# Attention and feed-forward on one core: copies of normalised rows issued last in their slot, raw heads in a head's first slot, v a slot later

## The chip, the cores and the metric

The kernel runs on one core of one Trainium2 chip. The metric is the device time of one execution in microseconds (us); lower is better. A core has five engines that run at the same time and meet through semaphores: TensorE (PE, matrix products; its weight loads are listed as PEld), VectorE (DVE), ScalarE (ACT), GpSimd (POOL) and SyncE (SP), which here issues every DMA, in the order in which the program lists them. If the next DMA in SP's list has to wait for a semaphore, all those behind it wait too.

## The reference

Decaying causal attention for 8 batches of 8 heads (576 tokens, head size 64), followed by a feed-forward block on the normalised rows:

```python
scores = scale * np.matmul(q, k.transpose(0, 1, 3, 2))
cum = np.cumsum(np.log(np.clip(f, 0.0001, 1.0)), axis=-1)
decay = cum[:, :, :, None] - cum[:, :, None, :]
scores = np.where(causal, -1000000000.0, scores + decay)
attn = np.exp(scores - np.max(scores, axis=-1, keepdims=True))
attn = attn / (np.sum(attn, axis=-1, keepdims=True) + 1e-09)
x = np.matmul(attn, v)          # then heads side by side: 4608 rows of 512
xn = (x - mu) / np.sqrt(var + 1e-06) * g_ln
out = x + np.maximum(xn @ w_ch1, 0.0) @ w_ch2
```

`w_ch1` and `w_ch2` come as float64. Everything else is float32.

## The kernel before

**Slots.** The 64 heads are worked off in 256 slots, four to a head: slot (n, t), with t from 1 to 4, computes the scores of one block of 128 query rows of head n (t = 1 takes the 64 rows ahead of it as well). A slot is a string of letters, and each letter is a piece of program: the list `ORDERS` (L53) gives the order for slots 0 to 36, 37 to 69 and from 70 on. Since every engine runs its own instructions in program order, this string also sets the order on each engine's queue. From slot 70 on it reads `WwDAthQFlMSPNgreamLRB`.

**What the letters issue.** `Q` is the score product (PE); `S` takes scores from PSUM into a row buffer `p` and finds the row extreme (DVE, L398); `e` is the exponential (ACT, L409); `B` divides the rows by their sums (two small DVE instructions, L414 and L415, then POOL, L416). `D` calls `move` (L426): from head 18 on SP copies the normalised rows of the slot before from `p` to a buffer `pq`, 32 to 288 KB a copy, five copies to a head (L431). `t`, `h` and `l` transpose the rows of the slot four before (PE), and split them into a high and a low part (ACT, DVE; L492, L497); heads below 18 do it two slots after. `A` multiplies them with v (PE, L527), one slot after the transposes; `F` and `a` add the halves and send the result to DRAM (L574). `M`, `r`, `m` and `N` are one step of the feed-forward: `M` the first product (PE, L604 to L606), `r` the Relu (ACT, L612), `m` its low part (DVE, L617), `N` the second product of the step before (PE, L626 to L628). `R` loads and splits what the feed-forward needs next: pieces of x (`xr`, split in L588 and L589) and rows for the residual (`xw`), all from L637; in some slots that is a train of eight and more DMAs. `N` also sends finished rows out (L687). `W`, `w`, `g` and `L` are pieces of the weights' preparation (in the first slots) and of small row statistics. Ahead of the letters, each slot loads the low part of a piece of the second weight (`w2s`, L719).

**What `P` issues** (`prep`, L867). In slot (n, t) it prepares head n + 1: t = 1 loads two rows of `kl` and rounds the raw k on ACT (L341, in `prep_a`); t = 2 subtracts on POOL (L344) and rounds the raw q on ACT (L348); t = 3 copies 64 rounded rows to `xq` by DMA (L351) and subtracts on POOL (L352). In slot (n, 4) it loads the raw q and k of head n + 2 (`start_head`, L323, 576 KB, from head 8 on; two buffers in turn). In the slot in which a head's first rows are transposed it rounds that head's v on DVE and POOL (`prep_v`, L358 and L359, from head 12 on), and right behind that it loads the next head's v (`load_v`, L331, 160 KB; from head 12 on into one and the same buffer, below that into two in turn).

**Buffers that matter here.** The row buffer `p` has three copies, one to a slot, so DVE's L398 writes a buffer again three slots after it was filled; it must then have been copied to `pq`. `pq` has nine.

**Overlap.** The feed-forward runs beside the attention from slot 35 on as far as rows and weights are there; what is left of its 288 steps runs alone when the heads are done, from about 1040 us on.

Of the kernel before, what the change touches and what calls it, by code (L numbers as in the profile page):

```python
# [15 lines left out]
B, H, S, D = 8, 8, 576, 64  # L16
# [10 lines left out]
NPLAIN = 8  # L27
# [25 lines left out]
ORDERS = [  # L53
    (0, "WwbQsSthAeMrgFmlLNPaRf"),
    (37, "WwbQSstAMhPelgLNFrfmBRa"),
    (70, "WwDAthQFlMSPNgreamLRB"),
]


# [1 line left out]
def attn_moe(ctx: ExitStack, tc: tile.TileContext, qk, v, f, g, w1, w2, out):  # L61
# [264 lines left out]
    def load_v(h):  # L326
        if h.full and h.n % 2 == 1:
            h.vr = work.tile([P, 5, 2, D], F32, tag="vv", bufs=1, name=f"vr{h.n}")[:, :, 0, :]
        else:
            h.vr = work.tile([P, 5, D], F32, tag="vr", bufs=1, name=f"vr{h.n}")  # L330
        nc.sync.dma_start(out=h.vr, in_=v[h.n])  # L331
# [31 lines left out]
    def qk_mm(h, t):  # L363
        q0, m, w = QT[t]
        cuts = [(0, w)] if w <= 512 else [(0, w // 2), (w // 2, w)]
        h.s = getattr(h, "s", {})
        h.s[t] = []
        for i, (a, z) in enumerate(cuts):
            sp = bank(f"s{h.n}_{t}_{i}")[:m, : z - a]
            xq, kl = h.xq[:, q0 : q0 + m], h.kl[:, a:z]  # L370
            if h.plain:
                mm(sp, xq, kl, start=True, stop=True)
            else:
                mm(sp, h.hi[:, 0, q0 : q0 + m], h.hi[:, 1, a:z], start=True, stop=False)  # L374
                mm(sp, xq, kl, start=False, stop=True)  # L375
            h.s[t].append((a, z, sp))
# [11 lines left out]
    def softmax_a(h, t):  # L388
        q0, m, w = QT[t]
        nm = f"{h.n}_{t}"  # L390
        if t == 0:
            pt = corner(h.n)
        else:
            pt = work.tile([P, S], F32, tag="p", bufs=3, name=f"p{nm}")
        st = work.tile([P, 4], F32, tag="st", bufs=6, name=f"st{nm}")
        off = S - P - (w - m)
        for i, (a, z, sp) in enumerate(h.s[t]):
            nc.vector.tensor_tensor_reduce(  # L398
                out=pt[:m, a:z], in0=sp, in1=mask[:m, off + a : off + z], scale=-SCALE,
                scalar=3.0e38 if i == 0 else st[:m, 0:1], op0=ALU.add, op1=ALU.min, accum_out=st[:m, i : i + 1],  # L400
            )
        h.p = getattr(h, "p", {})
        h.p[t] = (pt, st)

    def softmax_e(h, t):
        q0, m, w = QT[t]
        pt, st = h.p[t]
        i = len(h.s[t]) - 1
        nc.scalar.activation(pt[:m, :w], pt[:m, :w], AF.Exp, bias=st[:m, i : i + 1], scale=-1.0, accum_out=st[:m, 2:3])  # L409
# [80 lines left out]
    def transposed_hi(h, t):  # L490
        for tp, hi, lo in h.parts:
            nc.scalar.copy(out=hi, in_=tp)  # L492

    def transposed_lo(h):
        if not h.full:
            for tp, hi, lo in h.parts:
                nc.vector.tensor_tensor(out=lo, in0=tp, in1=hi.bitcast(F32), op=ALU.subtract)  # L497
# [50 lines left out]
    def finish(h):  # L548
        po, w, c0 = h.o
        b, hh = divmod(h.n, H)  # L550
        pr, j = divmod(hh, 2)
        g1 = c0 == 0
        if j == 0:
            xs_tile[g1] = work.tile([P, w], F32, tag="xs1" if g1 else "xs2", bufs=1, name=f"xs{h.n}_{c0}")
        xs = xs_tile[g1]
        js = slice(64 * j, 64 * j + 64)
        if h.full:
            nc.scalar.copy(out=xs[js, :], in_=po[0:64, :w])
        else:
            tmp = late.tile([P, S1], F32, tag="ot", bufs=1, name=f"ot{h.n}_{c0}")  # L560
            nc.scalar.copy(out=tmp[js, :w], in_=po[64:128, :w])
            h.tmp = tmp
        h.xs = xs

    def finish_add(h):
        po, w, c0 = h.o
        b, hh = divmod(h.n, H)
        pr, j = divmod(hh, 2)
        g1, xs = c0 == 0, h.xs
        js = slice(64 * j, 64 * j + 64)  # L570
        if not h.full:
            nc.vector.tensor_tensor(out=xs[js, :], in0=po[0:64, :w], in1=h.tmp[js, :w], op=ALU.add)
        if j == 1:
            nc.sync.dma_start(out=(xd1 if g1 else xd2)[b][P * pr : P * pr + P, :], in_=xs)  # L574
# [198 lines left out]
    hd = {}  # L773

    def start_head(n):
        hd[n] = load(n)
# [9 lines left out]
    for u, slot in enumerate(slots):  # L786

        def before(k):
            return slots[u - k] if u >= k else None

        if slot is not None:
            n, t = slot
            h = hd[n]
        def turn(more):

            for lag in (LAG, LAG_MOVED):
                b = before(lag + more)
                if b is not None and hd[b[0]].lag == lag:
                    return b
            return None  # L800

        av, av_t = None, 0
        if turn(1) is not None and turn(1)[1] in (2, 4):
            av, av_t = hd[turn(1)[0]], turn(1)[1]
        moe.fetch_low(ALL if wp.done() else wp.ready())
        want = moe.can(wp.ready()) and u >= FIRST_MOE

        def piece(c):
            tu = turn(0)
            if c == "t" and tu is not None:  # L810
                transpose_unit(hd[tu[0]], tu[1])
            elif c == "h" and tu is not None:
                transposed_hi(hd[tu[0]], tu[1])
            elif c == "l" and tu is not None:
                transposed_lo(hd[tu[0]])
            elif c == "Q" and slot is not None:
                if t == 1:
                    qk_mm(h, 0)
                qk_mm(h, t)
            elif c == "A" and av is not None:  # L820
                av_unit(av, av_t)
            elif c == "S" and slot is not None:
                if t == 1:
                    softmax_a(h, 0)
                softmax_a(h, t)
            elif c == "e" and slot is not None:
                if t == 1:
                    softmax_e(h, 0)
                softmax_e(h, t)
            elif c in FILL:  # L830
                wp.fill(FILL[c])
            elif c == "s":
                wp.sums()
            elif c == "F" and av is not None:
                finish(av)
            elif c == "a" and av is not None:
                finish_add(av)
            elif c == "r" and want:
                moe.first_high()
            elif c == "R":  # L840
                moe.limit = min(NCHUNK, max(0, u - (LAG if u < 4 * MOVED else LAG_MOVED) - 1) // (4 * H) * S // C)
                moe.rest()
            elif c == "L":
                run_later(RSTD)
            elif c == "M" and want:
                moe.first()
            elif c == "B" and slot is not None:
                normalise(h, t)
            elif c == "D":
                if before(1) is not None and hd[before(1)[0]].n >= MOVED:  # L850
                    move(hd[before(1)[0]], before(1)[1])
            elif c == "b" and before(1) is not None:
                b_n, b_t = before(1)
                if not hd[b_n].normal.get(b_t):
                    normalise(hd[b_n], b_t)
            elif c == "m" and want:
                moe.first_low()
            elif c == "W":
                due = 1 + min(u, W_CHANGE) / W_SLOTS + max(0, u - W_CHANGE) * W_TICKS
                while not wp.done() and wp.tick_no <= due:  # L860
                    wp.tick()
            elif c == "N":
                moe.second()
            elif c == "P":
                prep()

        def prep():  # L867

            if slot is not None:
                if t == 1 and n + 1 < NPLAIN:  # L870
                    start_head(n + 1)
                if NPLAIN <= n + 1 < B * H:
                    if t == 1:
                        prep_a(hd[n + 1])
                    if t == 2:
                        prep_b(hd[n + 1])
                    if t == 3:
                        prep_c(hd[n + 1])
                if t == 4 and NPLAIN <= n + 2 < B * H:
                    start_head(n + 2)  # L880
            first = turn(0)
            if first is not None and first[1] == 1:
                m = first[0]
                if not hd[m].full:
                    prep_v(hd[m])
                if m + 1 < B * H:
                    load_v(hd[m + 1])

        for c in [o for first, o in ORDERS if first <= u][-1]:
            piece(c)  # L890
# [48 lines left out]
```

## Time and profile before

| what | value |
|---|---|
| median of 3 runs | 1246.01 us (1243.95 to 1248.18) |
| the profiled execution | 1246.79 us, of which its span is 1245.0 us |
| mean granted TensorE clock | 0.982 |
| PE busy | 1203.7 us (97% of the span) |
| PEld, weight loads | 1069.0 us (86%) |
| DVE / ACT / POOL busy | 756.8 / 642.3 / 426.0 us |
| DMA | 228.5 MB, mean 184 GB/s |

How to read what follows. A row of waits says who waited for whom, with the total in us, the number of waits and the longest. A row of the timeline has its start in us from the span's start, its length in us, the engine, the line of the kernel, the operation, what it writes and reads, and in brackets the idle time of the engine just before it and what ended that. SPq is SP's queue: such a row is the issue of a DMA, not the transfer. A row of the windows has a stretch, its length, the busy time and count of instructions of each engine, the granted clock of PE as a share of full speed, the DMA engines' share and the rate.

### The profile page before, as it was taken

How to read it: one execution, taken by the hardware profiler on the slowest of the kernel's cores; microseconds unless marked ns; L12 is line 12 of the kernel's file. 1: busy time of each engine (PE TensorE's matmuls, PEld its weight loads, DVE VectorE, ACT ScalarE, POOL GpSimd, SP SyncE). 2: the span in 40 equal slices, each digit the busy share in tenths (PEclk: the TensorE clock that was granted, in tenths of full speed). 3: DMA queues.
4: the chain of work that ended last, by engine and by line, in shares of the span. 5: the costliest groups of instructions: out<-in, count | busy, mean ns of one | idle time of the engine just before them, and what ended most of it. 6: DMA issues, size and time to landing. Idle time of an engine off the chain costs nothing.

```text
span 1245.0 us, 26040 instructions
## 1 busy us (share of the span) xinstructions
PE 1203.7 (97%) x8140; PEld 1069.0 (86%) x8140; DVE 756.8 (61%) x2884; ACT 642.3 (52%) x1920; POOL 426.0 (34%) x533
## 2 busy tenths in 40 slices
PE   7998999999999989999999999999989999999998
PEld 5666889888898879889999989998989999999997
DVE  5777646575767666566767676766666774233232
ACT  5887655455555555455555565555545553112111
POOL 3667534333343334233434443443434330000000
PEclk8998999899999999989999999999999999999999
DMA  6888554356666656556667666766666654434433
GB/s 172 247 247 255 176 161 153 99 162 200 212 203 199 192 171 215 175 187 202 217 191 222 205 207 196 221 187 209 209 182 215 199 190 132 130 125 118 153 111 93
DMA packets 171482, 228.51 MB, mean 184 GB/s; under 512 B 40784, under 2 KB 107856, under 8 KB 171344
## 3 DMA queue, kind: packets, MB, share of 16 engines
q1 hardware_dynamic: 171344, 226.85, 59.2%
q8 instruction: 65, 1.06, 0.4%
q14 instruction: 73, 0.60, 0.2%
HBM read 157.46 MB, written 23.36 MB: 145 GB/s over the span
## 4 chain that ended last, share of the span: by engine, by line
PE 52%; DMA 5%; DVE 2%; ACT 2%; SPq 1%; issue 1%; DVEq 0%; ACTq 0%; POOLq 0%; POOL 0%
PE h L605 7%; PE h L604 7%; PE h L606 7%; PE acc L626 7%; PE acc L627 7%; PE acc L628 7%; DMA raw<-in_qk_dram 4%; PE o L527 4%; PE s L374 2%; PE tr L440 2%; PE s L375 2%; ACT p L409 1%; SPq L637 1%; DMA xr<-xb 1%; PE xp L649 0%
## 5 line engine op out<-in xcount | busy, mean ns | idle before, releaser
L416 POOL TENSOR_SCALAR p<-p,st 64x64 f32<-64x64 f32 (+4 forms) x320 | 173.4, 544 | 530.4 <-DVE st L415 226.0
L604 PE MATMUL h<-x,w1h 128*128 128x256 f32 x1152 | 331.3, 288 | 6.1 <-ACT x L588 3.3
L605 PE MATMUL h<-x,w1h 128*128 128x256 f32 x1152 | 327.3, 284 | 1.2 <-DVE st L414 0.7
L606 PE MATMUL h<-x,w1l 128*128 128x256 f32 x1152 | 326.4, 283 | 0.0
L617 DVE SCALAR_TENSOR_TENSOR hh<-h,hh 128x256 fp32r<-128x256 f32 x288 | 121.2, 421 | 222.6 <-ACT hh L612 217.5
L612 ACT ACTIVATE hh<-h 128x256 fp32r<-128x256 f32 x288 | 110.4, 383 | 268.5 <-PE h L606 265.1
L626 PE MATMUL acc<-w2h,hh 128*128 128x512 f32 x576 | 229.1, 398 | 12.8 <-ACT hh L612 12.8
L604 PEld LDWEIGHTS h<-x,w1h 128*128 128x128 f32 x1152 | 219.9, 191 | 12.2 <-ACT x L588 4.4
L627 PE MATMUL acc<-w2s,hh 128*128 128x512 f32 x576 | 228.2, 396 | 0.0
L628 PE MATMUL acc<-w2h,hh 128*128 128x512 f32 x576 | 226.8, 394 | 0.0
L605 PEld LDWEIGHTS h<-x,w1h 128*128 128x128 f32 x1152 | 220.3, 191 | 6.2 <-DVE x L589 2.7
L606 PEld LDWEIGHTS h<-x,w1l 128*128 128x128 f32 x1152 | 220.3, 191 | 0.0
L409 ACT ACTIVATE p<-p,st 64x64 f32<-64x64 f32 (+4 forms) x320 | 178.3, 558 | 73.4 <-DVE st L398 64.5
L492 ACT CAST ph<-tr 64x128 fp32r<-64x128 f32 (+4 forms) x416 | 117.7, 332 | 103.4 <-PE tr L440 53.2
L398 DVE CUSTOM_DVE_ANT_0 p<-s,mask 64x64 f32<-64x64 f32 (+4 forms) x320 | 130.4, 420 | 14.0 <-PE s L375 4.0
L626 PEld LDWEIGHTS acc<-w2h,hh 128*128 128x128 f32 x576 | 110.1, 191 | 26.6 <-ACT hh L612 14.0
L628 PEld LDWEIGHTS acc<-w2h,hh 128*128 128x128 f32 x576 | 109.3, 190 | 25.1 <-DVE st L414 0.5
L627 PEld LDWEIGHTS acc<-w2s,hh 128*128 128x128 f32 x576 | 110.3, 192 | 11.9
L497 DVE TENSOR_TENSOR ph<-tr,ph 64x192 fp32r<-64x192 f32 x208 | 62.6, 301 | 92.1 <-ACT ph L492 65.4
L374 PE MATMUL s<-hi 128*64 128x64 f32 x336 | 106.4, 339 | 0.3 <-DVE st L398 0.3
L375 PE MATMUL s<-kl,xq 66*64 66x64 f32 x336 | 98.6, 298 | 0.7 <-DMA xq<-hi 0.7
L497 DVE TENSOR_TENSOR pl<-tr,ph 128x128 fp32r<-128x128 f32 x208 | 95.2, 458 | 4.6
(86 smaller groups left out, 1796.0 us busy)
## 6 DMA issues: line engine op xcount, KB each, us to landing
w2s<-w2d SPq DMA_DIRECT2D x288, 256.0 KB
raw<-in_qk_dram SPq DMA_DIRECT2D x56, 576.0 KB
wr<-in_w_dram SPq DMA_DIRECT2D x32, 512.0 KB
pq<-p SPq DMA_DIRECT2D x46, 288.0 KB
pq<-p SPq DMA_DIRECT2D x46, 224.0 KB
vr<-in_v_dram SPq DMA_DIRECT2D x64, 160.0 KB
out_dram<-xt SPq DMA_DIRECT2D x36, 256.0 KB
xq<-hi SPq DMA_DIRECT2D x56, 144.0 KB
```

What stands on the lines that cost most here:

```text
L374: mm(sp, h.hi[:, 0, q0 : q0 + m], h.hi[:, 1, a:z], start=True, stop=False)
L375: mm(sp, xq, kl, start=False, stop=True)
L398: nc.vector.tensor_tensor_reduce(out=pt[:m, a:z], in0=sp, in1=mask[:m, off + a : off + z], scale=-SCALE, scalar=3.0e38 if i == 0 else st[: ...
L409: nc.scalar.activation(pt[:m, :w], pt[:m, :w], AF.Exp, bias=st[:m, i : i + 1], scale=-1.0, accum_out=st[:m, 2:3])
L416: nc.gpsimd.tensor_scalar(out=pt[:m, :w], in0=pt[:m, :w], scalar1=st[:m, 3:4], scalar2=1.0, op0=ALU.mult, op1=ALU.mult)
L497: nc.vector.tensor_tensor(out=lo, in0=tp, in1=hi.bitcast(F32), op=ALU.subtract)
L604: mm(ph, w1h[:, k, fs], c.x[k][:, 0, :], start=(k == 0), stop=False)
L605: mm(ph, w1h[:, k, fs], c.x[k][:, 1, :], start=False, stop=False)
L606: mm(ph, w1l[:, k, fs], c.x[k][:, 0, :], start=False, stop=(k == KT - 1))
L626: mm(c.acc[i], h[:, 0, ts_], w2h[:, j, :], start=(j == 0), stop=False)
L627: mm(c.acc[i], h[:, 0, ts_], low, start=False, stop=False)
L628: mm(c.acc[i], h[:, 1, ts_], w2h[:, j, :], start=False, stop=(j == FT - 1))
```

## The change

Three things are moved; no instruction is added or taken away. The letter `D` goes from third place to the last but one, behind `R`, so that SP issues a slot's copies of normalised rows behind that slot's other DMAs. The load of the raw heads goes from slot (n, 4) to slot (n, 1), from head 10 on, behind `prep_a`. The load of the next v goes one slot further back, out of the slot that rounds the current one.

```diff
-    (70, "WwDAthQFlMSPNgreamLRB"),
+    (70, "WwAthQFlMSPNgreamLRDB"),
...
-                if t == 4 and NPLAIN <= n + 2 < B * H:
+                if t == (4 if n + 2 < NPLAIN + 2 else 1) and NPLAIN <= n + 2 < B * H:
                     start_head(n + 2)
             first = turn(0)
             if first is not None and first[1] == 1:
                 m = first[0]
                 if not hd[m].full:
                     prep_v(hd[m])
-                if m + 1 < B * H:
-                    load_v(hd[m + 1])
+            second = turn(1)
+            if second is not None and second[1] == 1 and second[0] + 1 < B * H:
+                load_v(hd[second[0] + 1])
```

`turn(0)` is the slot whose rows are transposed now, `turn(1)` the one before it.

## Prediction

> **What bounds the kernel now.** I began with the page's chain of waits, to see whether anything but TensorE (PE) carries the end.
>
> ```profile
> PE 52%; DMA 5%; DVE 2%; ACT 2%; SPq 1%; issue 1%; DVEq 0%; ACTq 0%; POOLq 0%; POOL 0%
> PE h L605 7%; PE h L604 7%; PE h L606 7%; PE acc L626 7%; PE acc L627 7%; PE acc L628 7%; DMA raw<-in_qk_dram 4%; PE o L527 4%; PE s L374 2%; PE tr L440 2%; PE s L375 2%; ACT p L409 1%; SPq L637 1%; DMA xr<-xb 1%; PE xp L649 0%
> ```
>
> PE carries it, and the largest entry that is no matmul is the load of the raw heads: 4% of 1245 us, about 50 us. Next I asked who waits for that load, and what PE itself waits for: two answers of the waits view (total us, times, longest).
>
> ```profile
> ACT hi L341 <- DMA raw<-in_qk_dram: 82.7, 39, 6.5
> ```
>
> ```profile
> PE acc L626 <- ACT hh L612: 12.8, 6, 3.2
> PE tr L442 <- POOL p L416: 7.8, 5, 2.4
> PE h L604 <- ACT x L588: 3.3, 4, 2.2
> PE h L604 <- DVE st L414: 2.8, 1, 2.8
> PE o L527 <- DVE ph L497: 2.6, 4, 1.4
> ```
>
> ScalarE (ACT) waits 82.7 us for raw heads, but PE stops only now and then. The timeline shows how the one becomes the other.
>
> ```profile
> 516.17 0.43 SPq L637 DMA_DIRECT2D xw<-xb  x1
> ...
> 517.19 0.47 SPq L431 DMA_DIRECT2D pq<-p  x1
> ...
> 517.71 0.59 SPq L323 DMA_DIRECT2D raw<-in_qk_dram  x1
> ...
> 525.11 0.67 ACT L341 CAST hi<-raw 128x576 fp32r<-128x576 f32 x1 [6.50 <-DMA raw<-in_qk_dram]
> ...
> 526.25 0.80 PE L626 MATMUL acc<-w2h,hh 128*128 128x512 f32 x1 [3.07 <-ACT hh L612]
> ```
>
> The SP queue comes to the raw load late, behind a train of xw loads and a copy of normalised rows. The load takes 7.4 us (517.71 to 525.11). ACT stands at the cast, which is queued ahead of the Relu (L612), and PE stops 3.07 us for that Relu. All six L626 stops stand like this, just behind an ACT wait for raw; here are the first and the last of them:
>
> ```profile
> 322.38 0.67 ACT L341 CAST hi<-raw 128x576 fp32r<-128x576 f32 x1 [4.35 <-DMA raw<-in_qk_dram]
> 323.51 0.50 PE L626 MATMUL acc<-w2h,hh 128*128 128x512 f32 x1 [0.28 <-ACT hh L612]
> ```
>
> ```profile
> 919.45 0.67 ACT L341 CAST hi<-raw 128x576 fp32r<-128x576 f32 x1 [5.37 <-DMA raw<-in_qk_dram]
> 920.59 0.50 PE L626 MATMUL acc<-w2h,hh 128*128 128x512 f32 x1 [3.14 <-ACT hh L612]
> ```
>
> Last, the stages: those with such stops, and one quiet stretch (556 to 735) as the yardstick.
>
> ```profile
> core 0: us, PE busy (x) PEld busy (x) DVE busy (x) ACT busy (x) POOL busy (x), PEclk, DMA share, GB/s
> 235.00:250.00 15.00, 12.22 (x68) 10.70 (x66) 6.69 (x24) 6.91 (x21) 5.18 (x7) 0.77 0.32 103
> 250.00:330.00 80.00, 77.11 (x540) 69.38 (x539) 54.49 (x218) 44.14 (x135) 30.15 (x39) 1.00 0.61 185
> 390.00:412.00 22.00, 17.88 (x116) 15.67 (x114) 15.05 (x58) 11.06 (x36) 8.91 (x11) 0.92 0.63 191
> 450.00:465.00 15.00, 11.54 (x82) 10.06 (x80) 8.18 (x33) 6.79 (x22) 4.81 (x7) 1.00 0.58 181
> 520.00:535.00 15.00, 11.81 (x64) 9.91 (x62) 7.56 (x31) 6.61 (x20) 4.80 (x6) 0.77 0.51 161
> 535.00:556.00 21.00, 18.39 (x114) 16.62 (x113) 13.81 (x54) 10.27 (x32) 6.96 (x9) 0.84 0.62 192
> 556.00:735.00 179.00, 178.93 (x1302) 164.88 (x1301) 123.86 (x495) 105.37 (x319) 70.76 (x89) 1.00 0.67 210
> 840.00:860.00 20.00, 18.03 (x133) 16.21 (x132) 11.79 (x46) 9.94 (x32) 6.36 (x8) 1.00 0.71 213
> 915.00:927.00 12.00, 8.86 (x54) 7.82 (x54) 6.38 (x26) 5.38 (x17) 4.93 (x7) 0.86 0.65 202
> ```
>
> In the quiet stretch PE is never idle and starts 1302/179 = 7.27 matmuls per us. In the others it starts fewer, and five of them also show a granted clock of 0.77 to 0.92.
>
> **The change, part by part.**
>
> *Raw heads in slot 1.* The same 56 loads; from head 10 on each is issued three slots earlier, in front of that slot's R loads. The cast then finds its data, and the ACT wait goes. What PE lost to it I count twice. By named stops: the six L626 stops, 12.8; the L604 stop behind DVE, which in the first of these stages follows such an ACT wait too, 2.8; the longest of L604 behind x, 2.2, and the longest of L527, 1.4, both in stages with a late raw head: 19.2 us. To that the clock: 15 x 0.23 + 22 x 0.08 + 15 x 0.23 + 21 x 0.16 + 12 x 0.14 = 3.5 + 1.8 + 3.5 + 3.4 + 1.7 = 13.9 us, since the low clock stands only in stages with stops. Together 33 us. By rate: each stage's length less its matmuls over 7.27: 5.6 + 5.7 + 6.0 + 3.7 + 6.2 + 5.3 + 1.7 + 4.6 = 38.8 us. That is the most that these stages can give back; 33 is what raw heads explain.
>
> [...]
>
> What is next late there? The load writes a buffer that GpSimd (POOL) last read for the head two before. It is free long before the new place, as slot (32, 3) and the issue in the first slot of head 33 show, so SP should not stand on it:
>
> ```profile
> 509.07 1.43 POOL L352 TENSOR_TENSOR hi<-raw,hi 64x576 fp32r<-64x576 f32 x1
> ...
> 519.83 0.39 SPq L340 DMA_DIRECT2D kl<-cumd  x1
> ```
>
> *Copies last in their slot.* The 230 copies (46 heads, five each) remain; each is moved on SP past the slot's kl, raw, v, xq, xs, out and R issues. SP no longer stands on POOL with these behind it.
>
> ```profile
> SPq L431 <- POOL p L416: 226.5, 134, 7.2
> ...
> SPq L331 <- POOL vv L359: 57.8, 36, 5.5
> ...
> SPq L331 <- PE o L505: 28.9, 9, 7.5
> ```
>
> The first row's 226.5 us do not become a gain: SP is not the bound, and what it held back shows in PE's stops. I add 1 us for x loads that come earlier (L604 behind x, 3.3 less the 2.2 counted). The price: a copy must land before VectorE (DVE) writes that row buffer again, three slots after it was filled. How long does a copy take? It moves 32 to 288 KB. The nearest rows are a 576 KB load without a crowd, and an x piece of at most 128 KB behind a train of loads:
>
> ```profile
> 796.14 0.58 SPq L323 DMA_DIRECT2D raw<-in_qk_dram  x1
> ...
> 800.04 0.67 ACT L341 CAST hi<-raw 128x576 fp32r<-128x576 f32 x1 [1.07 <-DMA raw<-in_qk_dram]
> ```
>
> ```profile
> 841.07 0.43 SPq L637 DMA_DIRECT2D xr<-xa  x1
> ...
> 843.13 0.41 ACT L588 CAST x<-xr 128x256 fp32r<-128x256 f32 x1 [3.14 <-DMA xr<-xa]
> ```
>
> So 2.1 to 3.9 us; I take 2.5, near the smaller, whose size is nearer. Time left for it, from the end of the slot's last SP issue to the DVE write, in a common slot and in the tightest that I found:
>
> ```profile
> 578.09 0.42 SPq L637 DMA_DIRECT2D xr<-xa  x1
> ...
> 583.52 0.61 DVE L398 CUSTOM_DVE_ANT_0 p<-s,mask 128x448 f32<-128x448 f32 x1
> ```
>
> ```profile
> 593.26 1.57 SPq L637 DMA_DIRECT2D xr<-xa  x1
> ...
> 595.81 0.48 DVE L398 CUSTOM_DVE_ANT_0 p<-s,mask 128x320 f32<-128x320 f32 x1
> ```
>
> 5.0 us and 1.0 us. In the tight slots DVE would wait 1.5 us (up to 2.9). Of the 184 slots with copies I found four with under 2.5 us left. Part of such a wait hides, as most ACT waits for raw do, so I charge half: 4 x 1.5 / 2 = 3 us; at 3.9 us a copy, some 6 us.
>
> *v one slot later.* The 64 loads leave SP after the readers of their buffer are done, so the second and third row above (86.7 us of SP) mostly vanish. v is used a whole head later, so it stays covered; were that cover gone, the rounding on DVE would wait a load of 160 KB, 2 to 4 us, in each of 52 heads. No gain is charged: after 250 us it is inside the 33, and in the weight-preparing first 120 us, where transposes wait for POOL (7.8 us above), it may be worth -3 to +4.
>
> **Sum.** 33 + 1 - 3 = 31, with the early part's middle of +0.5 some 32 us. The profiled execution took 1246.8 us (span 1245.0): 1246.8 - 32 = 1214.8. The median of the runs is 0.8 lower, so 1214. With the bounds: 33 + 1 - 6 - 3 = 25 gives 1221; 38.8 + 4 - 1 = 42 gives 1204.
>
> **Rivals.** *Half of it: the trains of loads take raw's place.* The stops of 390 to 412, 520 to 556, 840 to 860 and 915 to 927 us come where SP issues eight or more xw and xr loads in a row at 0.43 us and more each. If x pieces and copies, now behind these trains, are late as the raw heads were, only the other stages give (5.6 + 5.7 + 3.7 = 15 us): 1231. For: L604 already waits for x. Against: its total is 3.3 us.
>
> *Slower: row buffers come free too late.* In slot 1 the copy now follows 576 KB of raw head. If it took 8 us, as the load at 517.71 nearly did, DVE would miss the 5.0 us of a common slot by 3 in each of 46 heads. ACT waits average 2.1 us (82.7/39) while PE stopped in only few of them, so 2 us hide; 46 x 1 = 46 us against the gain of 33: 13 slower, 1259. It decides from 7.7 us a copy. Against: raw has 3.9 us in quiet, and SP reaches it before it stands on POOL. [...]
>
> *Nothing: SP stands on the raw buffer in slot 1, or the stops were the trains' alone.* Then loads wait as now and the time stays within 3.7 us (0.3%, about what a measurement of this kernel can tell from no change).
>
> **Chances.** Forecast, 1204 to 1223: 0.72. Half, 1224 to 1238: 0.15. More than the stages' count: 0.03. Nothing: 0.04. Slower: 0.06. So faster 0.90, same 0.04, slower 0.06. From 1203 to 1231 holds the forecast and half of the second case: 0.8.
>
> **What would show it.** Right: L341 behind raw falls from 82.7 to under 5 us; L626 behind hh from 12.8 to under 3; the clock in 500 to 560 us is 1.00; SP's waits for vv and o are near nothing; SP still waits for POOL at L431. A new DVE wait at L398 for pq copies should total under 15 us. Wrong: that wait above 50 us, SP waiting at L323 for POOL, or the stops staying with xr or xw named.

## The result, and the profile after

The changed kernel takes 1206.21 us (median of 4 runs, 1205.75 to 1206.35), the kernel before 1244.98 us on the same chip. The ratio is 0.9696, 95% interval 0.9652 to 0.974: 38 us less, where 32 had been forecast and 1214 us named. (Gains here and below are one less the ratio, times 1245 us; the two medians differ by 38.8.) The profiled spans are 1245.0 before and 1204.0 after.

The page's chain of waits of the changed kernel:

```profile
PE 92%; DVE 3%; ACT 2%; DMA 2%; issue 1%; SPq 0%; POOL 0%; DVEq 0%; ACTq 0%; POOLq 0%
PE h L604 11%; PE h L605 11%; PE h L606 11%; PE acc L626 11%; PE acc L627 11%; PE acc L628 11%; PE o L527 6%; PE s L374 4%; PE tr L440 4%; PE s L375 3%; PE o L505 3%; PE tr L442 2%; PE s L372 2%; PE xp L649 1%; PE pc L191 1%
```

The load of the raw heads has gone from the chain. The chain is now PE for 92%, where it was 52%. What PE still waits for, in the changed kernel (total us, times, longest):

```profile
PE tr L442 <- POOL p L416: 6.0, 5, 2.3
...
PE h L605 <- DVE st L414: 1.3, 2, 1.1
...
PE o L527 <- DVE ph L497: 0.6, 2, 0.4
```

The row that stood first before, L626 behind the Relu with 12.8 us, is absent, and no row of ACT's waits names the cast behind a raw load. The first row is from the first 120 us. The rows of DVE and SP on which the prediction had set its marks:

```profile
DVE p L398 <- DMA pq<-p: 5.2, 4, 3.3
```

```profile
SPq L431 <- POOL p L416: 108.2, 77, 3.2
...
SPq L331 <- POOL vv L359: 17.7, 18, 1.5
SPq L331 <- PE o L505: 6.6, 4, 3.9
```

DVE does wait for a copy to leave its row buffer now, in four places and for 5.2 us. SP still stands on POOL at the copies, for half of what it was, and for v 24.3 us instead of 86.7; at the raw load (L323) it waits once, for 0.3 us. Two of the marks were missed: the waits for v are not near nothing, and the clock in 500 to 560 us is 0.97 and not 1.00, since 515 to 535 us still has a low stretch (below). Nor does SP stand much less in all: its waits add up to 681 us before and 650 after, since its wait for DVE at L574, where the attention's results go out, grew from 28.0 to 117.3 us.

Where the time came from can be read off one instruction that both kernels have in every head: ACT's cast of the raw k. Before, for heads 15, 18, 36, 53 and 63:

```profile
201.40 0.67 ACT L341 CAST hi<-raw 128x576 fp32r<-128x576 f32 x1 [0.77 <-DMA raw<-in_qk_dram]
256.93 0.67 ACT L341 CAST hi<-raw 128x576 fp32r<-128x576 f32 x1 [1.40 <-DMA raw<-in_qk_dram]
559.92 0.67 ACT L341 CAST hi<-raw 128x576 fp32r<-128x576 f32 x1
830.47 0.67 ACT L341 CAST hi<-raw 128x576 fp32r<-128x576 f32 x1
998.82 0.67 ACT L341 CAST hi<-raw 128x576 fp32r<-128x576 f32 x1 [1.41 <-DMA raw<-in_qk_dram]
```

And after, for the same heads:

```profile
197.95 0.68 ACT L341 CAST hi<-raw 128x576 fp32r<-128x576 f32 x1
246.87 0.68 ACT L341 CAST hi<-raw 128x576 fp32r<-128x576 f32 x1
529.48 0.67 ACT L341 CAST hi<-raw 128x576 fp32r<-128x576 f32 x1
798.28 0.67 ACT L341 CAST hi<-raw 128x576 fp32r<-128x576 f32 x1
956.96 0.67 ACT L341 CAST hi<-raw 128x576 fp32r<-128x576 f32 x1
```

The lead grows from 3.5 us (201.40 - 197.95) to 10.1, 30.4, 32.2 and 41.9. Between heads 36 and 53, 270 us in which PE had hardly stopped before, it grows by 1.8 us; all the rest falls in the stretches with stops. Those stretches now run at the pace of the quiet ones, but for one (windows of the changed kernel):

```profile
250.00:330.00 80.00, 79.56 (x570) 73.01 (x568) 58.57 (x229) 47.63 (x145) 34.60 (x44) 1.00 0.65 205
500.00:515.00 15.00, 14.88 (x103) 13.07 (x101) 13.09 (x55) 9.20 (x31) 6.33 (x8) 1.00 0.67 212
515.00:535.00 20.00, 18.39 (x116) 16.37 (x117) 12.86 (x52) 10.39 (x32) 8.41 (x12) 0.91 0.75 245
535.00:700.00 165.00, 165.00 (x1204) 152.34 (x1203) 115.24 (x452) 97.53 (x295) 66.06 (x83) 1.00 0.67 210
```

570/80 = 7.1 and 1204/165 = 7.3 matmuls per us; only 515 to 535 us is left at 5.8.

### The profile page after: what moved, and what is told of

It reads as the page before. It is cut to its first block, busy times and chain, and to the rows that moved or that the text cites. A ratio compares the mean times of both kernels' runs of the same rounds, so it can differ in the third digit from the quotient of the medians.

```text
span 1204.0 us, 25987 instructions
## 1 busy us (share of the span) xinstructions
PE 1185.4 (98%) x8140; PEld 1057.7 (88%) x8140; DVE 756.5 (63%) x2884; ACT 643.2 (53%) x1920; POOL 426.1 (35%) x533
## 3 DMA queue, kind: packets, MB, share of 16 engines
q8 instruction: 65, 1.06, 0.4%
## 4 chain that ended last, share of the span: by engine, by line
PE 92%; DVE 3%; ACT 2%; DMA 2%; issue 1%; SPq 0%; POOL 0%; DVEq 0%; ACTq 0%; POOLq 0%
PE h L604 11%; PE h L605 11%; PE h L606 11%; PE acc L626 11%; PE acc L627 11%; PE acc L628 11%; PE o L527 6%; PE s L374 4%; PE tr L440 4%; PE s L375 3%; PE o L505 3%; PE tr L442 2%; PE s L372 2%; PE xp L649 1%; PE pc L191 1%
## 5 line engine op out<-in xcount | busy, mean ns | idle before, releaser
L605 PE MATMUL h<-x,w1h 128*128 128x256 f32 x1152 | 325.6, 283 | 1.4 <-DVE st L414 1.3
L626 PE MATMUL acc<-w2h,hh 128*128 128x512 f32 x576 | 226.6, 393 | 0.0
L627 PE MATMUL acc<-w2s,hh 128*128 128x512 f32 x576 | 226.4, 393 | 0.0
L605 PEld LDWEIGHTS h<-x,w1h 128*128 128x128 f32 x1152 | 219.2, 190 | 5.2 <-DVE x L589 2.0
L626 PEld LDWEIGHTS acc<-w2h,hh 128*128 128x128 f32 x576 | 109.4, 190 | 12.6
L627 PEld LDWEIGHTS acc<-w2s,hh 128*128 128x128 f32 x576 | 109.3, 190 | 11.8
```

Of the source, the lines that this page charges most:

```text
L605: mm(ph, w1h[:, k, fs], c.x[k][:, 1, :], start=False, stop=False)
L626: mm(c.acc[i], h[:, 0, ts_], w2h[:, j, :], start=(j == 0), stop=False)
L627: mm(c.acc[i], h[:, 0, ts_], low, start=False, stop=False)
```

## The experiments

The theory: PE stopped because ACT stood at the cast of a raw head that came late, and all three moves help only as far as they bring that load forward. It had one refinement: PE does not feel the first few us of such a stand. The rivals: SP standing on POOL costs time whatever stands behind it; the copies' late place costs through the row buffers; and each us of ACT's standing costs its share, against the refinement.

**Each part alone.** The first kernel has only the raw load moved:

```diff
-                if t == 4 and NPLAIN <= n + 2 < B * H:
+                if t == (4 if n + 2 < NPLAIN + 2 else 1) and NPLAIN <= n + 2 < B * H:
```

> Only the raw heads are moved to slot 1; copies stay third in their slot and v stays where it was. If late raw heads cause the stops of PE: 1245 less the 33 of the prediction, 1209 to 1218, ACT's wait at L341 for raw under 5 us, the stops of L626 gone, SP's wait for POOL at L431 still above 150 us. If it is SP standing on POOL that costs the time, whatever stands behind it: less than 15 us of gain, 1230 or more, with the stops moved to x or w2s loads.

It took 1208.67 us, ratio 0.9723 (0.9696 to 0.9749): 34 us. Its waits name a raw load at L341 once, with 0.7 us, and no stop of L626. SP stands on POOL nearly as long as before, without harm:

```profile
SPq L431 <- POOL p L416: 210.5, 125, 4.5
...
SPq L331 <- POOL vv L359: 48.8, 35, 5.5
```

So the theory holds (the time is 0.3 us under its range), and SP's standing as such is not the cost. The second kernel has only the copies moved:

```diff
-    (70, "WwDAthQFlMSPNgreamLRB"),
+    (70, "WwAthQFlMSPNgreamLRDB"),
```

> Only the copies go last in their slot; raw heads stay in slot 4, v where it was. If late raw heads are the cause, a raw load now comes earlier by one issue and one wait for POOL (0.5 + 226.5/134 = 2.2 us), so the waits at L341 under 2.2 us go and the long ones shrink by as much: a gain of 10 to 18 us, 1228 to 1236, L341 still waiting 20 to 40 us. If SP standing on POOL is the cause: 30 us or more, 1216 or less.

1223.37 us, ratio 0.9839 (0.9812 to 0.9866): 20 us, between the two expectations. ACT still stands for more than the 20 to 40 us that the theory had allowed:

```profile
ACT hi L341 <- DMA raw<-in_qk_dram: 45.1, 28, 4.9
```

```profile
PE acc L626 <- ACT hh L612: 1.7, 3, 1.0
```

ACT's standing fell by less than half (82.7 to 45.1), PE's stops behind it by seven eighths (12.8 to 1.7). The long waits were what PE felt, and shortening them by some us is enough to end most of the stops behind the Relu. SP now stood at v instead (L331 behind POOL 131.5 us, 57.8 before). The third kernel has only v moved (the last part of the diff).

> Only v goes a slot later. If late raw heads are the cause: SP's waits for vv and o at L331 (86.7 us) go, and the gain is 0 to 6 us, most of it in the first 130 us: 1239 to 1245. If SP's freedom in itself is worth time: 12 us or more, 1233 or less.

1229.84 us (1225.84 to 1236.98), ratio 0.9881 (0.9841 to 0.9922): 15 us. That is not the theory's 0 to 6 us but inside the range of its rival, that SP's freedom in itself is worth time. The four runs spread over 11 us; the profiled one, the longest of them with a span of 1235.2 us, shows 10 us of gain:

```profile
ACT hi L341 <- DMA raw<-in_qk_dram: 75.9, 39, 6.4
```

```profile
PE acc L626 <- ACT hh L612: 11.9, 7, 3.0
```

In it the stop of 2.8 us in 235 to 250 us is gone, and most of the others stand. The gain starts there: the raw load of head 17 is no longer late, as its cast shows, before and with v moved.

```profile
236.56 0.67 ACT L341 CAST hi<-raw 128x576 fp32r<-128x576 f32 x1 [3.81 <-DMA raw<-in_qk_dram]
```

```profile
232.29 0.67 ACT L341 CAST hi<-raw 128x576 fp32r<-128x576 f32 x1
```

By head 20 the lead is 7.1 of the 9.9 us that it has at head 63. And SP is no freer at the copies: it stands there for 250.0 us, against 226.5 before. So the profiled run speaks for the theory's path, with a larger gain than expected; what the other three runs, 4 to 11 us shorter, gained beyond it no profile shows, and the rival is refuted by the kernel with raw alone and not by this one.

34 + 20 + 15 = 69 us, for a change worth 38: the gains overlap, as they must if the three cure the same waits. The two kernels with one part left out say the same. Raw and v, with the copies in their old place:

> Raw heads and v are moved, the copies stay third in their slot: the whole change less its first part. If the copies' place is worth little either way once raw heads are early: 1204 to 1209, within 3 us of the whole change. If a late copy place pays through earlier x and raw loads: 1212 or more. If it costs through the row buffers: 1203 or less, with the stop near 515 us of the changed kernel gone.

1205.87 us, ratio 0.9699 (0.9671 to 0.9727): the whole change's time, so the copies' place, this one or the old one, is worth nothing that the measurement can tell once the raw load is early. A stop near 515 us stays with the copies in their old place too. Copies and v, with the raw load in slot 4:

> The whole change without its raw part: copies last, v later, raw heads still in slot 4. If PE feels only what goes beyond about 2 us of ACT standing at L341, the two parts together shorten the waits below that nearly everywhere: 1209 to 1217, with ACT still waiting 15 to 40 us for raw. If the early place of the raw load is what counts: 1220 or more, as with the copies alone.

1214.44 us, ratio 0.9751 (0.9715 to 0.9786), inside the range of the first expectation:

```profile
ACT hi L341 <- DMA raw<-in_qk_dram: 28.1, 20, 4.4
```

```profile
PE acc L626 <- ACT hh L612: 2.1, 2, 1.2
```

**How much standing of ACT is free?** In the changed kernel ACT repeats the cast of L341, so that it is held at that place for a known time in each of 56 heads:

```diff
-        nc.scalar.copy(out=h.hi[:, 1, :], in_=h.raw[:, 1, :])
+        for _ in range(3 + 1):
+            nc.scalar.copy(out=h.hi[:, 1, :], in_=h.raw[:, 1, :])
```

> The changed kernel, and ACT repeats the cast of L341 three times more in each head (the result is the same): 3 x 0.67 = 2.0 us in which ACT is held at the place where it used to wait for raw heads. If PE only feels what goes beyond about 3 us there: no change to speak of, 1204 to 1213. If each us of holding ACT costs its share, as the 82.7 us of waits cost some 35 us: 56 x 2.0 x 0.4 = 45 us, 1245 to 1255.

> The same with six casts more, 4.0 us a head. If PE feels what goes beyond about 3 us: 56 x 1 = 56 us and low clock on top, 1255 to 1300. If in proportion: 56 x 4.0 x 0.4 = 90 us, 1290 to 1300, and twice the cost of three casts. If ACT simply has room (it is busy 53% of the span): 1215 or less.

Three more casts: 1227.47 us, ratio 0.9864 (0.9833 to 0.9896). Six more: 1342.8 us, ratio 1.0778 (1.0746 to 1.081). Against the changed kernel's 1206.2 the first 2.0 us a head cost 21 us, the next 2.0 us cost 115. That is no proportion, and no room either. Both times lie outside all the ranges expected: the first between them, the second above them. PE's waits with three and with six (one line has been added, so L627 is the L626 of before):

```profile
PE h L605 <- ACT x L589: 6.9, 9, 1.7
...
PE o L506 <- ACT ph L493: 2.7, 2, 1.4
```

```profile
PE acc L627 <- ACT hh L613: 47.4, 41, 2.5
PE h L605 <- ACT x L589: 23.8, 9, 3.8
```

With six casts the old stop is back, 41 times. Two windows, the first of three casts, the second of six, show the pace:

```profile
535.00:700.00 165.00, 163.53 (x1177) 150.03 (x1176) 112.61 (x444) 114.96 (x321) 64.32 (x81) 1.00 0.65 205
```

```profile
600.00:1100.00 500.00, 457.64 (x3145) 409.98 (x3144) 305.56 (x1205) 363.83 (x951) 174.44 (x220) 0.97 0.57 181
```

1177/165 = 7.13 and 3145/500 = 6.29 against 7.30 matmuls per us. In the changed kernel a head lasts 15.9 us at these places ((956.96 - 798.28)/10), so the head is longer by 0.4 us for 2.0 us of holding and by 2.6 us for 4.0. About 1.5 us a head are free, not the 3 us that I had expected (by the whole times, 21 and 136 us over 56 heads, 1.6 us both times).

This figure can be held against the kernels in which ACT's waits were real ones. Before, it waited for raw at 39 of the casts, and what these waits exceed 1.5 us by adds up to 33 us. In the profiled run with v moved 28 of that are left, with the copies moved 14, with copies and v 7, and with raw alone nothing: 5, 19, 26 and 33 us less. The spans of these four runs are 10, 25, 32 and 38 us shorter than before. That is 5 to 6 us more in each, and the same steps from one kernel to the next. So one path, ACT's standing beyond about 1.5 us, sorts all three moves; the 5 to 6 us that all four share it leaves open.

**How early must the load be?** The changed kernel with the raw load in slot 3:

```diff
-                if t == (4 if n + 2 < NPLAIN + 2 else 1) and NPLAIN <= n + 2 < B * H:
+                if t == (4 if n + 2 < NPLAIN + 2 else 3) and NPLAIN <= n + 2 < B * H:
```

> The changed kernel with the raw load in slot 3 instead of slot 1, one slot (about 4 us) ahead of where it was. If waits of under 3 us are free: the longest wait of before, 6.5 us, falls under that, 1204 to 1210 and some ACT waits for raw of 1 to 3 us. If the load has to be well ahead of the trains: 1214 or more, with L626 stops again.

1206.24 us, ratio 0.9693 (0.966 to 0.9726). Beside the other two moves one slot is as good as three; ACT's waits for raw come to 1.5 us in all.

```profile
ACT hi L341 <- DMA raw<-in_qk_dram: 1.5, 3, 0.7
```

**When do late copies decide?** The changed kernel with each copy one slot later still:

```diff
-                if before(1) is not None and hd[before(1)[0]].n >= MOVED:
-                    move(hd[before(1)[0]], before(1)[1])
+                if before(2) is not None and hd[before(2)[0]].n >= MOVED:
+                    move(hd[before(2)[0]], before(2)[1])
```

> The changed kernel with the copies one slot later still (end of the second slot after the rows' own). Of the 5.0 us left to a copy in a common slot some 1 us remains. If the row buffer then decides, as the prediction's slower rival has it with copies of about 2.5 us: DVE waits 1.5 us and more at L398 for pq copies in each of 184 slots, well over 100 us of waits, and the time is 1230 or more. If copies are so quick, or DVE so free, that it never binds: 1204 to 1212.

1250.63 us (1243.17 to 1257.73), ratio 1.0046 (1.0021 to 1.0071): 44 us slower than the changed kernel, and no faster than before. The rival's mechanism is real, one slot away from where the change stands:

```profile
DVE p L398 <- DMA pq<-p: 101.6, 63, 4.2
```

```profile
PE tr L440 <- DMA pq<-p: 20.3, 20, 3.1
```

DVE waits in 63 places, not in 184, and PE's transposes now wait for copies too; which of the two makes the 44 us was not separated.

**Copies ahead of the trains.** The remaining 5.2 us of DVE waits should go if the copies stand before `L` and `R`:

```diff
-    (70, "WwAthQFlMSPNgreamLRDB"),
+    (70, "WwAthQFlMSPNgreamDLRB"),
```

> The whole change with the copies just ahead of the trains (D before L and R) instead of behind them. The waits of DVE at L398 for copies (5.2 us in four) should go. If they cost nothing, as no stop of PE names them: 1204 to 1208. If the copies' lateness costs: 1203 or less.

> The same with the raw load in slot 3: the two places together that looked mildest. If nothing in these three places matters any more once ACT no longer stands at L341: 1204 to 1208. If one of them still costs: 1203 or less.

With the raw load in slot 1: 1205.09 us, ratio 0.9677 (0.9635 to 0.9719). With it in slot 3: 1208.85 us, ratio 0.971 (0.9676 to 0.9745), 0.85 us beyond what was expected; the intervals overlap. Neither is a better kernel than the changed one by more than the measurement can tell. The waits did not go: in the first of the two kernels two are left, at the places of the two longest in the changed kernel, and they cost nothing that the whole time shows:

```profile
DVE p L398 <- DMA pq<-p: 3.7, 2, 2.8
```

## Why the prediction was right, point by point

- **What bounds the kernel, and the path from a late raw load to a stop of PE:** right. The raw load alone gives 34 us of the 38, and holding ACT by hand at the cast brings the stop of L626 back.
- **The size of that term, 33 us by named stops or 38.8 by rate:** 34 for the raw load alone, 38 for the whole. I took the lower count for the raw heads, and that was right. The count by rate came nearer to the whole, but in part by luck: 3.5 us of the changed kernel's lead arose before the first of its stages, and stage by stage it was off by up to 4 us (520 to 556 us promised 11.5 and gave about 8). The 6 us between the 32 forecast and the 38 measured would be made up by the 3 charged to the copies and some 3 more in the early part.
- **3 us charged for copies that come late:** nothing that shows in the time, by the kernel with the copies in their old place (1205.87 against 1206.21 us). DVE's waits came (5.2 us, under the 15 named), but PE's one stop for a copy is 0.2 us long.
- **No gain from v, but for -3 to +4 in the first 120 us:** right only inside the whole, where v adds 3 us to the raw load's gain (1208.67 to 1205.87), with intervals that overlap. Alone it gives 15, against 0 to 6 expected of it.
- **The early part:** the changed kernel leads by 3.5 us at head 15, and I had set the middle at 0.5 and given it to v. It is the raw load again: with that alone the cast of head 15 starts at 198.00 us, against 197.95 for the whole change. By which wait these first 3.5 us came was not tried.

```profile
198.00 0.68 ACT L341 CAST hi<-raw 128x576 fp32r<-128x576 f32 x1
```

- **"SP is not the bound":** right, since SP stood on POOL for 210.5 us in the kernel with raw alone. But what I expected of the copies alone, 10 to 18 us, was too low (20 us): nearly all of what lies beyond 1.5 us a head counts, and the copies' move takes 19 us of the 33.
- **The slower rival:** it did not come about, but its mechanism does decide one slot later. My margin of 5.0 us in a common slot was about right in size: less one slot of 4 us, the copies bind in 63 of the 184 slots.
- **The trains as the next bound:** refuted in size, since 38 us came and not 15. In the one stretch left with a stop (515 to 535 us) PE waits at a product with x (L605), with DVE named, and does so with the copies in either place; the cause was not tried.

## What to carry to other kernels

In this kernel a wait on a side engine cost the main one nothing until it was longer than the slack between them (about 1.5 us), and then nearly all of it (2.0 us of holding ACT made a head 0.4 us longer, 4.0 us made it 2.6 us longer): cure the longest waits, and expect several cures of the same waits to overlap, not to add (34, 20 and 15 us alone, 38 together). Here a large load, the 576 KB of raw heads, paid when it was issued further ahead of its use (34 us), and one slot further ahead was as good as three, beside the other two moves (1206.24 and 1206.21 us). To size the gain, count it more than one way: by listed stops, by the matmuls per us of the bad stretches against a good one, and, where the slack is known, by what each wait exceeds it by (here 33, 38.8 and 33 us, for 34 from the raw load and 38 in all).

## What the runs showed of the hardware that I had not expected

Whether a stop of PE is followed by a stretch at a granted clock of 0.50 was not set by its length alone in these runs. At the same place, with stops of nearly the same length (1.06 and 0.41 us, 1.04 and 0.41 us), the changed kernel lost the clock and the kernel with the copies ahead of the trains (raw load in slot 1) kept it. The changed kernel's two stops (its window of 515 to 535 us, at 0.91, stands above):

```profile
516.02 0.38 PE L605 MATMUL h<-x,w1h 128*128 128x256 f32 x1 [1.06 <-DVE st L414]
...
516.93 0.56 PE L527 MATMUL o<-ph,vv 128*128 128x320 f32 x3 [0.41 <-DVE ph L497]
```

The other kernel's two stops and its window:

```profile
516.01 0.38 PE L605 MATMUL h<-x,w1h 128*128 128x256 f32 x1 [1.04 <-DVE x L589]
...
516.92 0.56 PE L527 MATMUL o<-ph,vv 128*128 128x320 f32 x3 [0.41 <-DVE ph L497]
```

```profile
515.00:535.00 20.00, 17.36 (x121) 15.39 (x122) 12.93 (x52) 10.41 (x32) 8.66 (x13) 1.00 0.71 239
```

The kernel before kept its clock (450 to 465 us, at 1.00) through two longer stops:

```profile
457.80 0.50 PE L626 MATMUL acc<-w2h,hh 128*128 128x512 f32 x1 [2.07 <-ACT hh L612]
...
460.85 0.56 PE L527 MATMUL o<-ph,vv 128*128 128x320 f32 x3 [1.39 <-DVE ph L497]
```

In the changed kernel's window the low clock stands at 0.50 for 3.42 us, so by my estimate it costs about 1.7 us (half of that), as much as the 1.5 us of the stops.

```profile
517.78:521.20 3.42, 3.42 (x17) 3.34 (x16) 1.36 (x5) 1.49 (x5) 2.63 (x3) 0.50 1.00 379
```

It is not all that this window lost: DVE's longest wait for a copy falls there too.

```profile
523.08 0.62 DVE L398 CUSTOM_DVE_ANT_0 p<-s,mask 128x448 f32<-128x448 f32 x1 [3.33 <-DMA pq<-p]
```

The kernel that kept the clock has such a wait as well, of 2.8 us, and starts 121 matmuls against 116 in these 20 us; the kernel with raw in slot 3 has the full clock and no such wait, and starts 136:

```profile
515.00:535.00 20.00, 18.69 (x136) 16.92 (x135) 14.21 (x54) 11.99 (x38) 9.75 (x13) 1.00 0.75 239
```

So at this one place a late copy does seem to cost PE something, by a path that was not followed.

The kernel before has five stretches at 0.50 behind its first 120 us: 6.83 us from 238.77, 3.42 from 406.02, 6.83 from 525.49, 6.83 from 545.97 and 3.42 from 921.43 us. What decides whether a stop brings one was not shown: stops of 1.06 and 0.41 us were followed by it in the changed kernel, stops of 2.07 and 1.39 us were not in the kernel before.
